# Value-score products in 128x32 tiles for four of six chunks, a second load of the values, and a new order of steps

## The chip, the cores and the metric

The kernel runs on one core of one Trainium2 chip. The metric is device time in microseconds (us), the median of the runs shown. A profile is one execution, taken by the hardware profiler. Engines: PE is TensorE (PEld are its weight loads), DVE is VectorE, ACT is ScalarE, POOL is GpSimd, SP is SyncE, which here only issues transfers.

## The reference

A gated recurrence over time feeds a bilinear feed-forward layer:

```python
# q, k, v, alpha: (B, H, S, D) = (4, 8, 768, 48)
for t in range(S):
    state = alpha[:, :, t, :, None] * state + np.einsum('bhd,bhe->bhde', k[:, :, t], v[:, :, t])
    y[:, :, t] = np.einsum('bhd,bhde->bhe', q[:, :, t], state)
x = y.transpose(0, 2, 1, 3).reshape(3072, 384)
out = ((x @ w_a) * (x @ w_b)) @ w_out          # w_a, w_b: (384, 1536), w_out: (1536, 384)
```

Everything comes in and goes out in float32; the large products use bf16.

## The kernel before

The work is cut into six chunks. Chunk `c` holds two of the four batches (`u` is 0 or 1 for them) and 256 time steps, as 128 pairs of neighbouring tokens, one pair per partition. A token's place in its pair is its rank (`rk` 0 or 1). Each 256 steps are again two halves `g` of 64 partitions, with a state passed from half to half.

For a chunk the steps are, by the names of the program:

- `ld a/k/q/v`: loads. `ln` (`logs`, L556) takes the logarithm of alpha, `l2` adds the two of a pair, `R`, `H` and `L` split it for exact sums, `B`, `A2` or `AQ` build running sums on PE, `E` (`expo`, L667) makes exponentials of them (`E u i` the inverse), `ra` (L645) another exponential, `lv` (`level`, L652) multiplies the first token of each pair, `mk`/`mq` (L678) scale keys and queries into `QKp`.
- `C` turns `QKp` on PE with `Ce` as its copy out (L742 on ACT, L744 on DVE); later chunks turn by a DMA transpose, `T` (tile `kqT`). `dk`/`de` (L721) or `dr`/`dl` make the decays.
- `v` (`vcast`, L785 on ACT, L787 on DVE) copies the loaded values into the padded tile `vx`; `K`, `K2` (L799, L812) are the state products and `k` the state update.
- `D` (L841) makes the scores. `M` masks them on DVE while copying out of PSUM; `Mc` copies on ACT (L850) and `Mm` masks in place later (L854).
- `SB` and `SA` (`carried`) add the states' part of the output, `Y` (`inner`) the products of values with masked scores; both issue at L865 in 64x64 tiles. The result lies in two PSUM banks, one per half `g`. `X` (`evac`, L900 on ACT, L902 on DVE) copies it as `xT`.
- The feed-forward layer: `a f w bank` and `b f w bank` (`ff`, L919) are three matmuls each into the bank that is named, for slice `f` of 12, over one `u` (256 columns) or both (`*`, 512 columns). `as` (L925) copies an `a` result out on ACT, which frees its bank; `pr` (L933) multiplies it with the `b` result on DVE, which frees that bank. `o m half bank` (L941) is six matmuls of 384 columns with `w_out`; `ot` copies out, `st` stores.

A `Y` of one `u` is 48 matmuls: 12 pieces (a head's 48 outputs cut at multiples of 64) times two ranks times two halves. Each contracts 64 partitions and gives 64 output rows for 128 columns; four tiles of 64x64 are used in turn.

No scheduler orders the work. `PROGRAM` is a written list of all steps, chunk number first, and each engine executes its instructions in the order of that list; steps of chunk `c+1` and `c+2` stand between the feed-forward steps of chunk `c`. PE, ACT, DVE, POOL and SP each have such a queue, and a waiting instruction holds up all behind it on its engine. All PSUM banks are named by hand, so a matmul into a bank waits for the copy of what the bank held.

The step `c1a` (`const_table`, L468) loads ACT's function table `natural_log_exp_and_others`, which holds logarithm, exponential and copy. It is the first thing that ACT does.

Of the kernel before, what the change touches and what calls it, by code (L numbers as in the profile page):

```python
# [17 lines left out]
0: cm 0; c1; cz 0 b P; ci; ld a 0b Y; c1a; ld a 0a Y; ln 0b; cu; cz 1 b P; fill 7 2; cu2 V; cz 0 q V; cus; ld k 0b Y; ld k 0a Y; B 0b 5; ld q 0b Y; ld v 0 P  # L18
0: ln 0a; ld q 0a Y; E 0b b; E 0b i; mq 0b V; B 0a 0; E 0a i; dk 0 2; E 0a b; ld a 1 P; mk 0b V; C 0 1 5; cs 0 m P; ld k 1 P; ld q 1 P; v 0 S; mk 0a V; cm 1
0: de 0; fill 2 1; mq 0a V; C 0 0 3; Ce 0 1 V; W b 0 256; cz 0 v P; Ce 0 0 V; D 0 1 4; ln 1; ld v 1 P; W a 256 768; K 0 0 6; k 0 0 V; M 0 1; D 0 0 0; SB 0 6  # L20
0: cz 1 q P; B 1a 2; M 0 0; W a 0 256; E 1a i; E 1a b; W b 256 768; mq 1a V; mk 1a V; B 1b 4; dk 1 3; E 1b i; E 1b b; de 1; v 1 S; mq 1b V; mk 1b V; C 1 0 0
0: Y 0; SA 0; Ce 1 0 V; cs 1 m P
1: ld a 0 P; ld a 1 P
0: W a 768 1536; C 1 1 1; X 0 S; c2 P; D 1 0 3; W b 768 1536
1: ld q 0 P
0: Ce 1 1 V; K 1 0 5; k 1 0 V; a 4 0 0
1: ld k 0 P
0: D 1 1 6; SB 1 1
1: ld v 0 P; ld q 1 P
0: Mc 1 0; a 3 0 5; Wo 0 6; a 0 0 3; Mm 1 0 V; Mc 1 1; as 0 0; b 0 0 4  # L30
1: ld k 1 P
0: pr 0 0; b 1 0 6; a 2 0 3; a 1 0 7; a 5 0 4; as 2 0; b 2 0 3; Mm 1 1 V; as 1 0; b 4 0 7; as 5 0; b 5 0 4; pr 2 0; pr 1 0
1: ln 0
0: SA 1; Y 1; Wo 6 12; K 1 1 6; as 3 0; as 4 0; X 1 S
1: ra 0
0: K 0 1 3
1: l2 0 V
0: b 3 0 0; pr 5 0; pr 4 0
1: H 0 V; L 0 V
0: a 2 1 1; a 5 1 2; as 5 1; pr 3 0; a 1 1 7; b 4 1 5; b 5 1 4; as 2 1; k 0 1 V; pr 5 1; a 4 1 2; as 1 1  # L40
1: ln 1
0: b 2 1 0; pr 2 1; a 6 * 3; as 4 1; b 1 1 2
1: l2 1 V
0: pr 4 1; as 6 *
1: H 1 V
0: pr 1 1
1: A2 0 7
0: a 11 * 0; a 7 * 5; a 0 1 4
1: L 1 V
0: k 1 1 V  # L50
1: ra 1
0: as 11 *
1: lv 0 q V; E 0 i
0: as 0 1; b 6 * 0; b 11 * 3; a 8 * 4; pr 6 *; pr 11 *
2: ld a * P
0: b 0 1 1; as 8 *; a 3 1 6
1: E 0 b; lv 0 k V
0: a 10 * 2; pr 0 1
1: mq 0 V; ld v 1 P
0: b 8 * 4  # L60
1: A2 1 7
0: as 10 *; b 10 * 2; pr 8 *
1: E 1 b
0: as 3 1; as 7 *; b 9 * 3; b 3 1 0; b 7 * 1; a 9 * 6
2: ld q * P
1: v 0 S; lv 1 q V; mk 0 V
0: pr 10 *
1: mq 1 V; C 0 1 4
0: as 9 *
1: C 0 0 2  # L70
0: o 0 0 5; pr 7 *
1: dk * 6
2: ld k * P
3: ld v * P
0: cz 1 v P; pr 9 *
1: Ce 0 0 S; E 1 i; de *; lv 1 k P; Ce 0 1 V; D 0 1 1; D 0 0 3
0: pr 3 1
1: Mc 0 0; K2 0 0 7 0
0: o 1 0 6
1: mk 1 V; M 0 1  # L80
0: o 3 0 4; o 1 1 -; ot 1 S; c3 P
3: ld a * P
0: cs 1 0 P; o 3 1 -
1: k 0 0 V; k 0 1 V; Mm 0 0 V; SB 0 1; C 1 0 3; C 1 1 7
0: ot 3 S; o 0 1 -
1: Ce 1 0 V
2: ln *
1: v 1 V; D 1 0 3; Ce 1 1 S; K2 1 1 6 0; Y 0; SA 0
0: ot 0 V
1: k 1 0 V; D 1 1 6  # L90
0: o 2 0 5
1: M 1 0
2: l2 0 V
1: X 0 S; a 3 0 1; Mc 1 1
2: l2s 0 P; l2s 1 P
1: a 2 0 3; a 4 0 4
2: R 0
1: k 1 1 V; as 4 0
2: ra 1
1: as 3 0; b 4 0 7  # L100
0: o 2 1 -
1: as 2 0
0: ot 2 S
1: pr 4 0
2: R 1; lv 1 q P
1: b 3 0 6; b 2 0 7; a 5 0 2; pr 3 0; b 5 0 3; as 5 0; b 1 0 5; a 1 0 1; pr 5 0; pr 2 0; a 7 0 2; as 1 0; pr 1 0
2: AQ 3
1: SB 1 6
2: lv 0 k P
1: a 10 0 5  # L110
2: lv 1 k V; ra 0; ld v * P
1: Mm 1 1 V
2: E 1 b
1: as 10 0; b 10 0 0; pr 10 0
2: mq 1 V; E 1 i
1: as 7 0; b 7 0 1
2: E 0 b; E 0 i
1: a 0 0 5
0: st 3 Y
2: dr  # L120
1: SA 1; Y 1
2: mk 1 V
1: pr 7 0; a 11 0 0; a 6 0 3; b 6 0 2; X 1 S; b 11 0 4; a 2 1 6; as 6 0; a 3 1 7; as 11 0; b 2 1 1; pr 6 0
2: lv 0 q V
1: b 4 1 0; as 2 1
2: T 1
1: pr 11 0
2: dl
0: st 0 Y
1: a 0 1 2; pr 2 1  # L130
2: mq 0 V
1: b 3 1 3; b 0 0 6; as 3 1; as 0 0; b 0 1 7; pr 3 1; a 8 0 1; a 9 0 5
0: st 1 Y
1: b 8 0 3; b 9 0 4; pr 0 0; as 0 1
2: mk 0 V
1: a 4 1 2
3: ln *
1: a 9 1 6; pr 0 1; as 8 0; b 9 1 1
3: ra 1
1: b 10 1 7; pr 8 0; a 10 1 3; as 4 1; as 9 0; as 9 1; a 6 1 6; b 6 1 2; b 11 1 5; pr 4 1; as 10 1; pr 9 0; a 11 1 4; pr 10 1; pr 9 1; as 6 1  # L140
2: v 1 S
1: a 8 1 3; b 8 1 1; a 7 1 6; pr 6 1
3: l2 0 V
1: as 11 1
2: T 0
1: as 8 1; a 5 1 4
3: ra 0
1: as 5 1; a 1 1 2
2: v 0 V
4: ld a * Y  # L150
1: pr 11 1; as 7 1; pr 8 1
2: K2 * * 0 7; D 1 1 3; D 1 0 5
1: as 1 1; b 5 1 2; o 2 0 1
2: k * 0 V
1: pr 5 1
3: v 0 S; v 1 S
1: b 1 1 2
2: Mc 1 0; M 1 1
3: l2s 0 P; l2s 1 P
1: b 7 1 0; o 2 1 -; pr 1 1; o 3 0 4  # L160
2: SB 0 5
1: pr 7 1
3: R 0
2: D 0 0 2
1: ot 2 V
2: Mm 1 0 V
1: o 3 1 -
2: Mc 0 0; SB 1 0; D 0 1 2
3: R 1
1: ot 3 S  # L170
2: SA 0
1: o 0 0 4
0: cs 0 0 P
2: Mc 0 1
4: ln *
3: ld q * Y; ld k * Y
2: k * 1 V
3: AQ 2
2: Y 1; SA 1; Mm 0 1 V; Mm 0 0 V; Y 0; X 0 S
3: E 0 b  # L180
4: l2 0 V
2: X 1 V
1: o 0 1 -
2: b 1 * 6; a 1 * 5
3: E 1 b
4: ld k * Y
3: E 1 i
1: ot 0 S
3: E 0 i
4: l2s 0 P  # L190
2: a 0 * 0; b 0 * 1; as 0 *; as 1 *
3: lv 0 k P; lv 0 q P
2: a 5 * 7
1: st 3 Y
2: a 7 * 4
4: l2s 1 P
2: a 2 * 5
3: lv 1 q V; mq 1 V; lv 1 k V
2: pr 1 *
3: dr  # L200
2: pr 0 *
3: mk 0 V
4: ld q * Y
0: st 2 Y
2: as 5 *; a 6 * 6; b 6 * 2; as 7 *
3: mq 0 V
2: b 9 * 4; b 7 * 0
1: st 2 Y
3: dl
4: R 0  # L210
2: b 5 * 7
1: o 1 0 3
2: a 9 * 1; pr 7 *; as 6 *
3: T 0
2: pr 6 *
4: ra 0
2: pr 5 *; a 11 * 6
3: mk 1 V
2: as 9 *; a 3 * 0
4: lv 0 k V; lv 0 q V; R 1  # L220
2: as 2 *
1: o 1 1 -
2: as 11 *; a 8 * 5; b 11 * 2; a 4 * 7; b 2 * 1
3: T 1
1: ot 1 V
2: pr 9 *; as 8 *; pr 11 *; pr 2 *; b 8 * 3; b 4 * 5; as 4 *
5: ld a * Y
3: K2 * * 4 6
2: pr 8 *; as 3 *; pr 4 *
3: k * 0 V; D 0 0 2; Mc 0 0  # L230
2: b 3 * 1
4: ra 1
2: pr 3 *; b 10 * 5; a 10 * 0
3: D 1 0 1; D 1 1 3
2: as 10 *
3: k * 1 V; Mc 1 1
2: o 0 0 7; o 2 0 0
3: M 1 0
5: ln *
2: pr 10 *  # L240
4: lv 1 q P
3: SB 1 3; D 0 1 1; Mc 0 1
4: lv 1 k P
5: ld q * Y
1: st 0 Y
3: SB 0 5
2: o 2 1 -
3: Mm 1 1 V; Mm 0 0 V; Mm 0 1 V
4: ld v * P
2: ot 2 S; o 0 1 -  # L250
4: AQ 0; E 0 b; E 0 i
3: SA 0; Y 0; SA 1
4: E 1 b
3: Y 1
5: l2s 1 V
4: mq 0 V; mk 0 V
3: X 0 S; X 1 S
2: o 3 0 2; o 3 1 -
4: T 0
3: a 5 * 3  # L260
4: E 1 i; v 0 S
3: a 9 * 0
2: ot 3 S
3: b 5 * 6; a 6 * 5; as 5 *
2: st 2 Y
3: as 9 *
5: ld k * P; l2s 0 P
3: as 6 *
5: ra 1
4: mq 1 V  # L270
2: ot 0 S
3: a 0 * 1
4: mk 1 V
3: a 1 * 2
4: D 0 0 3
5: l2 0 V
1: st 1 Y
4: dr
5: R 0
3: pr 5 *  # L280
4: v 1 S; M 0 0
3: b 1 * 7; as 1 *; a 3 * 5; b 9 * 6; pr 9 *; b 6 * 4; a 2 * 0; pr 6 *
4: T 1
5: lv 0 k P
3: b 0 * 6; as 0 *; as 2 *
4: dl
3: a 8 * 1
5: lv 1 q P
3: b 4 * 0; a 4 * 4; b 2 * 3; pr 1 *; pr 0 *; as 8 *; pr 2 *; as 4 *; pr 4 *; b 3 * 6; b 8 * 2
5: ld v * P; lv 1 k P  # L290
3: a 11 * 1
5: ra 0
3: as 3 *; pr 8 *; as 11 *; a 7 * 0
4: D 1 0 3; K * 0 5
5: lv 0 q P
3: pr 3 *; as 7 *
5: v 1 V
4: k * 0 V
5: R 1
4: D 1 1 6; D 0 1 1; Mc 1 0; Mc 1 1; M 0 1  # L300
2: o 1 0 0; o 1 1 -
3: a 10 * 7; b 11 * 3
4: SB 1 4
2: ot 1 S
3: as 10 *
4: Mm 1 0 V
3: pr 11 *
4: SB 0 1
5: AQ 6; E 0 i; E 0 b; mk 0 V
3: b 10 * 0; b 7 * 3  # L310
4: Mm 1 1 V
5: mq 0 V
3: o 2 0 6; pr 7 *
4: Y 0; SA 0
3: pr 10 *
5: E 1 b
4: X 0 V; Y 1; SA 1
2: st 1 Y
3: o 1 0 3
4: X 1 S  # L320
3: o 2 1 -
5: E 1 i
4: a 7 * 2
5: mq 1 V
4: b 7 * 7; a 6 * 1; as 7 *; as 6 *
3: o 1 1 -
4: b 1 * 5; a 0 * 1; a 1 * 4
5: dr; T 0
2: st 3 Y
4: b 6 * 2  # L330
3: ot 2 V
4: pr 7 *; a 5 * 6
5: mk 1 V
3: ot 1 V
4: pr 6 *
5: v 0 S
4: as 0 *; as 1 *; pr 1 *
2: st 0 Y
5: T 1
4: b 0 * 7; as 5 *; pr 0 *; a 4 * 1; a 3 * 0  # L340
5: K * 0 2; dl
# [757 lines left out]
```

## Time and profile before

| | |
|---|---|
| runs | 194.41 us median of 3 (193.69 to 194.47) |
| span of the profiled execution | 192.0 us (first to last instruction; the page gives no other time of it) |
| PE busy | 186.8 us, 97% |
| DVE / ACT / POOL busy | 133.1 / 106.5 / 56.9 us |
| granted PE clock | 1.000 |
| DMA | 62618 packets, 29.40 MB |
| last matmul group | starts at 187.17 us |

Busy times of one engine's instructions may overlap: a matmul's mean of 217 ns is its time from entering to leaving, while the next ones follow some 14 ns apart. What a stage costs is therefore read from starts: from the first instruction of a group to the first of the next.

### The profile page before, as it was taken

The numbers are of one execution on the slowest core, as the hardware profiler recorded it, in microseconds if no ns is written. First come the engines' busy times: TensorE is split into PE (matmuls) and PEld (weight loads), VectorE is DVE, ScalarE is ACT, GpSimd is POOL, SyncE is SP. The second block draws the span as 40 slices with busy tenths as digits, with TensorE's granted clock in tenths as the row PEclk, the third lists the DMA queues.
The fourth block names the chain that finished last, engine by engine and source line by source line (L and its number), as shares of the span: only waits on it lengthen the run. The fifth ranks groups of instructions, "written<-read, shape, count | busy, mean of one in ns | idle before, by whom it ended". The sixth has DMA issues, their size and how long they took to land.

```text
span 192.0 us, 6086 instructions
## 1 busy us (share of the span) xinstructions
PE 186.8 (97%) x2613; PEld 116.9 (61%) x2613; DVE 133.1 (69%) x223; ACT 106.5 (55%) x194; POOL 56.9 (30%) x75
## 2 busy tenths in 40 slices
PE   7999999999999999999999999999999999999992
PEld 3888875677778876645557444656465644545562
DVE  2387698994989888899897956887567446252510
ACT  4448885656779867753487756743572435314211
POOL 8999626752450500640074262000000000000000
PEclk9999999999999999999999999999999999999999
DMA  5999999999969999999999989017641200000422
GB/s 132 274 219 218 251 253 235 244 269 264 251 107 166 165 216 265 248 254 149 233 213 181 156 174 129 3 42 140 146 66 44 85 0 0 0 0 3 164 82 82
DMA packets 62618, 29.40 MB, mean 153 GB/s; under 512 B 53712, under 2 KB 60768, under 8 KB 62592
## 3 DMA queue, kind: packets, MB, share of 16 engines
q0 software_dynamic: 18432, 13.37, 39.6%
q1 hardware_dynamic: 44016, 15.55, 38.1%
q8 instruction: 20, 0.33, 0.7%
q10 hardware_dynamic: 144, 0.10, 0.2%
q14 instruction: 6, 0.05, 0.1%
HBM read 25.98 MB, written 4.74 MB: 160 GB/s over the span
## 4 chain that ended last, share of the span: by engine, by line
PE 91%; DMA 5%; SPq 1%; DVE 1%; issue 1%; ACT 0%; DVEq 0%
PE psum L919 47%; PE psum L941 24%; PE psum L865 7%; PE psum L841 3%; DMA kqT<-QKp 3%; DMA q_t<-in_q_dram 3%; PE psum L736 2%; PE psum L633 1%; PE psum L952 1%; SPq L549 1%; PE psum L799 1%; PE psum L812 1%; PE psum L700 1%; PE psum L591 1%; PE psum L592 1%
## 5 line engine op out<-in xcount | busy, mean ns | idle before, releaser
L919 PE MATMUL psum<-xT,wb_t 128*128 128x512 bf16 (+1 forms) x270 | 56.0, 337 | 0.0
L919 PE MATMUL psum<-xT,wa_t 128*128 128x512 bf16 (+1 forms) x270 | 56.0, 337 | 0.0
L941 PE MATMUL psum<-wo_t,prod 128*128 128x384 bf16 x276 | 49.4, 326 | 0.0
L919 PEld LDWEIGHTS <-wb_t 128*128 128x128 bf16 x270 | 25.9, 98 | 19.9 <-issue 0.5
L919 PEld LDWEIGHTS <-wa_t 128*128 128x128 bf16 x270 | 25.9, 98 | 19.7 <-issue 0.3
L941 PEld LDWEIGHTS <-prod 128*128 128x128 bf16 x276 | 25.9, 98 | 17.6
L956 ACT ACTIVATE ot<-psum 128x384 f32<-128x384 f32 (+1 forms) x16 | 7.7, 482 | 22.7 <-PE psum L941 21.6
L850 ACT ACTIVATE m<-psum 128x1024 bf16<-128x1024 f32 x14 | 14.1, 1023 | 4.6 <-PE psum L841 4.3
L613 POOL TENSOR_TENSOR l<-la 64x384 f32<-64x384 f32 x7 | 7.8, 1108 | 26.6 <-ACT la L556 19.0
L846 DVE TENSOR_TENSOR m<-psum,mask 128x1024 bf16<-128x1024 f32 x10 | 12.1, 1220 | 3.1 <-PE psum L841 3.1
L652 POOL TENSOR_TENSOR q_t<-q_t,ra 128x384 f32<-128x384 f32 x5 | 6.1, 1215 | 22.5 <-ACT ra L645 19.7
L556 ACT ACTIVATE la<-a_t 128x1536 f32<-128x1536 f32 (+2 forms) x9 | 9.5, 1055 | 2.3 <-DMA a_t<-in_alpha_dram 2.2
L678 DVE TENSOR_TENSOR QKp<-q_t,beta 128x768 bf16<-128x768 f32 x10 | 10.0, 995 | 1.0 <-ACT beta L667 1.0
L865 PE MATMUL psum<-m,vx 64*64 64x128 bf16 x576 | 10.5, 217 | 0.0
L900 ACT ACTIVATE xT<-psum 128x768 bf16<-128x768 f32 x9 | 7.2, 816 | 5.7 <-PE psum L865 5.5
L678 DVE TENSOR_TENSOR QKp<-k_t,invb 128x768 bf16<-128x768 f32 x10 | 9.7, 972 | 0.8 <-ACT invb L667 0.8
L854 DVE TENSOR_TENSOR m<-m,mask 128x1024 bf16<-128x1024 bf16 x14 | 9.3, 684 | 1.2 <-ACT m L850 1.2
L958 DVE COPY ot<-psum 128x384 f32<-128x384 f32 (+1 forms) x9 | 4.8, 532 | 7.6 <-PE psum L941 4.7
L865 PEld LDWEIGHTS <-vx 64*64 64x64 bf16 x576 | 9.0, 107 | 0.5 <-issue 0.3
L841 PE MATMUL psum<-kqT 64*64 64x128 bf16 x384 | 9.0, 219 | 0.4 <-DMA kqT<-QKp 0.3
L652 POOL TENSOR_TENSOR k_t<-k_t,a_t 128x384 f32<-128x384 f32 x6 | 7.4, 1228 | 6.1 <-issue 3.3
L549 POOL DMA_DIRECT2D v_t<-in_v_dram x8 | 8.5, 1058 | 0.1
(271 smaller groups left out, 287.9 us busy)
## 6 DMA issues: line engine op xcount, KB each, us to landing
out_dram<-ot SPq DMA_DIRECT2D x23, 192.0 KB, 3.8
q_t<-in_q_dram SPq DMA_DIRECT2D x3, 768.0 KB, 6.5
a_t<-in_alpha_dram POOLq DMA_DIRECT2D x2, 768.0 KB, 15.2
k_t<-in_k_dram POOLq DMA_DIRECT2D x2, 768.0 KB, 12.1
v_t<-in_v_dram POOLq DMA_DIRECT2D x4, 384.0 KB, 7.0
a_t<-in_alpha_dram SPq DMA_DIRECT2D x2, 768.0 KB
k_t<-in_k_dram SPq DMA_DIRECT2D x2, 768.0 KB
a_t<-in_alpha_dram POOLq DMA_DIRECT2D x3, 384.0 KB, 8.5
```

Source lines behind the costliest of these rows:

```text
L549: eng.dma_start(out=t[:, us, hs].rearrange("p b h r d -> p (b h) (r d)"), in_=src[ch.b0 + us.start:ch.b0 + us.stop, hs, ch.s * 2 * C:(ch.s ...
L556: nc.scalar.activation(out=ch.la[:, us, hs].rearrange("p b h r d -> p (b h r d)"), in_=ch.a[:, us, hs].rearrange("p b h r d -> p (b h r d) ...
L613: eng.tensor_add(ch.l2[(1 - g) * HC:(2 - g) * HC, 1], x[:, :, 0, :], x[:, :, 1, :])
L652: eng.tensor_mul(x, x, by)
L678: eng.tensor_mul(QKp[ch.c % 2][:, u, j, :, hs, :D], src[:, u, hs].rearrange("p h r d -> p r h d"), f)
L841: nc.tensor.matmul(s2[g * HC:(g + 1) * HC, r, p, rk, :], lhsT=turned_part(ch, u, 1, rk, 2 * h + p, g, rs), rhs=queriesT(ch, u, 2 * h + p, ...
L846: nc.vector.tensor_mul(m.rearrange("p r a k s -> p (r a) (k s)"), ch.s2[u, h].rearrange("p r a k s -> p (r a) (k s)"), maskn(4))
L850: nc.scalar.activation(out=m.rearrange("p r a k s -> p (r a) (k s)"), in_=ch.s2[u, h].rearrange("p r a k s -> p (r a) (k s)"), func=AF.Copy)
L854: eng.tensor_mul(x, x, maskn(4))
L865: nc.tensor.matmul(y[c * DP:(c + 1) * DP, g, j // 2 * C:(j // 2 + 1) * C], lhsT=lhsT, rhs=rhs, start=(g, c) not in begun, stop=False, skip ...
L919: nc.tensor.matmul(p, lhsT=(wa_t, wb_t)[w][:, kk, f * 128:(f + 1) * 128], rhs=ch.xT[:, kk, us, :], start=(kk == 0), stop=(kk == KT - 1))
L941: nc.tensor.matmul(op, lhsT=ch.prod[:, f, at:at + C], rhs=wo_t[:, f, :], start=(f == 0), stop=(f == NFF - 1))
```

## The change

For chunks 2 to 5 (`NR = 2`), `Y` contracts over both ranks at once: 64 pairs times two ranks are 128 partitions, and an output piece is 32 rows, so the tiles are 128x32, four of them side by side. A `Y` of one `u` is then 16 slices times two halves, 32 matmuls, still of 128 columns. In all 256 matmuls stand where 384 were; chunks 0 and 1 keep theirs (192).

- The scores `D` of these chunks write their halves and ranks in the other arrangement (as many matmuls), with the mask `mask2`, built once from `mask` (`cm2`).
- `lw` (`load_rows`) loads the values a second time in that layout, into a reshaped view of `vx`: four loads per chunk on POOL's queue, 16 in all, each of 64 x 16 pieces of 48 elements. `cz 0 w` and `cz 1 w` zero the padding. `ld v` stays, for the state products, which now read it directly; `vcast` is gone for these chunks (nine on ACT and three on DVE become three and one).
- `evac` copies one half `g` at a time (24 copies of 128x384 in place of 12 of 128x768; ACT 13, DVE 11) and puts the tokens in their own order, so that `ff_prod` reads and writes without a permutation.
- `PROGRAM` is new throughout. Among much else, six `l2` additions move from DVE to POOL, three more of the `lv k` multiplications too, two more `Ce` copies go to ACT, and `Y` and `SA`/`SB` are grouped: over the whole program PE changes its tile size 58 times where it did 55 times.
- `c1a` now stands late in chunk 1's steps. The built program has 11 table loads on ACT where it had one: besides `c1a` itself, one ahead of `ln` in five places, and one ahead of `E` or `ra` in five places, in each case directly before that instruction in ACT's order.

The core of the diff, with the lines of the new list that matter here:

```diff
-0: cm 0; c1; cz 0 b P; ci; ld a 0b Y; c1a; ld a 0a Y; ln 0b; cu; cz 1 b P; fill 7 2; ...
+0: c1; cm 0; cz 0 b P; ci; cu; cu2 V; cus; ld a 0b Y; fill 7 0; ln 0b; B 0b 2; cz 1 b P; ...
+0: ... v 0 S; cs 0 m P; Ce 0 1 V
+0: C 0 0 1; Ce 0 0 V; cz 1 v P; ld k 1 P; K 0 0 2; de 0; ... SB 0 2; ln 1; W b 0 256; B 1a 6; E 1a i
...
+0: K 1 1 2; D 1 1 6; Mc 1 1; k 1 1 V; SB 1 0; a 0 0 3; as 0 0
+1: ld a 1 P
+0: b 0 0 4; a 3 0 5; b 1 0 2; a 1 0 6; as 1 0; a 4 0 3; as 4 0; Mm 1 0 V; Mm 1 1 V; Y 1; SA 1; W a 768 1536; X 1 1 S; X 1 0 V; pr 0 0; b 4 0 3; b 5 0 6; a 2 0 7
+0: b 1 1 0
+1: ln 0
+0: a 0 1 1; c2 P; W b 768 1536; as 0 1; pr 1 0; a 1 1 2; as 1 1; pr 4 0
+1: ld q 0 P
+0: a 5 0 4; as 5 0; b 0 1 1; pr 0 1; b 3 0 2; b 5 1 3
...
+0: o 3 1 -
+1: Mc 0 0
+2: ln *; l2s 1 P
...
+2: R 0; ra 1
+1: v 1 S; K2 1 1 6 7; k 1 0 V
+2: R 1
+1: Ce 1 0 S
...
+0: o 1 0 1
...
+1: b 5 0 3; b 10 0 4; a 11 0 5; pr 0 0; pr 10 0
+2: lw 0 0 P
+1: as 5 0; pr 5 0
+3: ln *
+1: X 1 0 V; b 9 0 2; b 3 0 1; as 9 0; a 2 0 6; as 2 0; a 4 0 4
...
+1: b 0 1 0; pr 9 0; a 2 1 7
...
+3: ra 1
...
+1: b 11 0 2; as 4 0; pr 4 0
+3: lw 0 0 P
+1: a 0 1 3; a 4 1 4; as 4 1; ...
...
+0: c1a; cz 0 w P
...
+    VP = D + DP // 2
+    NR = 2
...
+    vps = [t.rearrange("p b r h e -> p (b r h e)")[:, :4 * H * VP].rearrange("p (g b h e) -> p g b h e", g=2, b=2, h=H) for t in vxs]
...
+    def load_rows(ch, g, rk, eng):
+        at = ch.s * 2 * C + g * C
+        eng.dma_start(out=vps[ch.c % 2][rk * HC:(rk + 1) * HC, g, :, :, :D].rearrange("p b h d -> p (b h) d"),
+                      in_=v[ch.b0:ch.b0 + 2, :, at:at + C, :].rearrange("b h (s r) d -> r s (b h) d", r=2)[rk])
...
+    def values(ch, gs, u, rk, hd):
+        return ch.v[gs, u, hd, rk, :] if ch.c >= NR else vxs[ch.c % 2][gs, u, rk, hd, :D]
...
+    SLICES = [(h, 3 * (h // 2) + j) for h in range(H) for j in ((0, 1) if h % 2 == 0 else (1, 2))]
+    RANKS = [[x for x in SLICES if x[1] % 4 == c] for c in range(4)]
+
+    def inner_rows(ch, u):
+        y, begun = ch.y[u]
+        vp = vps[ch.c % 2].rearrange("p g b h e -> p g b (h e)")
+        W32 = DP // 2
+        for n in reversed(range(len(SLICES) // 4)):
+            for g in range(2):
+                for c in range(4):
+                    h, j = RANKS[c][n]
+                    at = h * VP + W32 * j - D * h
+                    nc.tensor.matmul(y[c * W32:(c + 1) * W32, g, j // 4 * C:(j // 4 + 1) * C], lhsT=vp[:, g, u, at:at + W32],
+                                     rhs=ch.m[u, h // 4][:, h % 2, h // 2 % 2, g, :], start=False, stop=False, skip_group_check=True)
+
     def inner(ch, u):
+        if ch.c >= NR:
+            return inner_rows(ch, u)
...
-    def evac(ch, u, eng):
+    def evac(ch, u, g, eng):
...
-        o_ = ch.xT[:, :, 2 * u:2 * u + 2, :].rearrange("p a g s -> p g a s")
-        i_ = ch.y[u][0][:, :, :KT * C].rearrange("p g (a s) -> p g a s", a=KT)
...
+        evict(ch.xT[:, :, 2 * u + g, :].rearrange("p a (s r) -> p a r s", r=2),
+              ch.y[u][0][:, g, :KT * C].rearrange("p (a r s) -> p a r s", a=KT, r=2), eng)
...
-        o_, a_, b_ = tokens(ch.prod[:, f, :], us), columns(a[:, :n], n), columns(b, n)
-        nc.vector.tensor_mul(o_, a_, b_)
+        nc.vector.tensor_mul(ch.prod[:, f, us.start * C:us.stop * C], a[:, :n], b)
```

## The prediction

> **What bounds the kernel now.** First the page: busy times, the slices, the chain.
>
> ```profile
> PE 186.8 (97%) x2613; PEld 116.9 (61%) x2613; DVE 133.1 (69%) x223; ACT 106.5 (55%) x194; POOL 56.9 (30%) x75
> ...
> PE   7999999999999999999999999999999999999992
> ...
> DMA  5999999999969999999999989017641200000422
> ...
> PE 91%; DMA 5%; SPq 1%; DVE 1%; issue 1%; ACT 0%; DVEq 0%
> ```
>
> PE carries the chain and has work in every slice after the first. What PE waited for, from the waits of PE alone, is almost nothing:
>
> ```profile
> PE psum L574 <- DVE og L472: 1.2, 1, 1.2
> PE psum L841 <- DMA kqT<-QKp: 0.3, 1, 0.3
> ```
>
> So a matmul less is time gained, and any new wait of PE is time lost, one for one: nothing gives it back. Prices are steps between starts. From the chain in order of time (start, length, what):
>
> ```profile
> 49.72 1.31 PE psum L919 x12
> ...
> 86.91 0.98 PE psum L941 x6
> ```
>
> 1.31/12 = 0.109 us per matmul of 256 columns, so 0.33 us for an `a` or `b` of one `u`; 0.98/6 = 0.163 us for 384 columns. From PE's timeline:
>
> ```profile
> 127.94 1.14 PE L941 MATMUL psum<-wo_t,prod 128*128 128x384 bf16 x6
> 129.01 0.87 PE L865 MATMUL psum<-m,vx 64*64 64x128 bf16 x48
> ...
> 129.87 0.84 PE L865 MATMUL psum<-m,vx 64*64 64x128 bf16 x48
> 130.54 0.22 PE L865 MATMUL psum<-kqT,S 64*64 64x128 bf16 x1
> ```
>
> The second `Y` takes 130.54 - 129.87 = 0.67 us: 14 ns per 64x64 matmul, 56 ns per four. A change of tile size costs 129.01 - 127.94 - 6 x 0.163 = 0.09 us. Last ACT, at the start and by groups:
>
> ```profile
> 0.73 1.28 ACT L468 ACT_TABLE_LOAD   x1 [0.73 <-PEq L1083]
> 3.62 1.14 ACT L556 ACTIVATE la<-a_t 128x384 f32<-128x384 f32 x2 [1.61 <-DMA a_t<-in_alpha_dram]
> 6.68 0.87 ACT L667 ACTIVATE prod<-psum 128x384 f32<-128x384 f32 x2 [1.92 <-PE psum L592]
> ...
> 10.80 0.84 ACT L556 ACTIVATE la<-a_t 128x768 f32<-128x768 f32 x1 [0.43 <-DMA a_t<-in_alpha_dram]
> ```
>
> ```profile
> L556 ACT ACTIVATE la<-a_t 128x1536 f32<-128x1536 f32 x4 | 5.9, 1476 | 0.0
> ...
> L700 PE MATMUL psum<-og,la 128*48 128x2 f32 x64 | 1.8, 186 | 0.0
> ```
>
> A table load is 1.28 us of ACT, and today's single one lies under the wait for alpha.
>
> **The products.** 384 matmuls become 256, each still of 128 columns. If four 128x32 tiles run side by side as four 64x64 tiles do, the step stays 14 ns: 128 x 14 ns = -1.8 us. No row has a 128x32 tile. The lower end is this price. For the upper end, L700 is the only row with full-height, column-cut tiles: 32 of them step at 26 ns (14.83 to 15.67 us), by which 256 cost 6.7 us against 5.4: +1.3. I take 14 ns: L700's weights are float32, and its streams are two columns.
>
> A rule that speaks against the edit: L941's weight loads take 98 ns each, all on the same 128 rows, and still its matmuls follow each other at 163 ns for 384 columns, so these loads hide. The Trainium skill (TensorE: Matmul & The Clock Gate, Part 3, The mechanism) says that a weight load overlaps running matmuls only where the row group differs, though it names the background buffer as a second way; 128-row tiles share all row groups. What exposed loads would cost stands below as a rival.
>
> Tile sizes change 58 times for 55: 3 x 0.09 = +0.3.
>
> **The table loads** are the largest term. With `c1a` late, ten more are put ahead of `ln`, `E` and `ra`, directly in ACT's queue, and behind each wait the `as` that free PE's banks. At each I ask which PE step needs the next ACT step. `as` is 0.38 us (128x256), `la` 0.84 or 1.48, `ra` and `E` 0.5.
> - Loads 1, 2 and 4, chunk 0: 1 replaces today's; 2 ends at 4.76 + 1.28 = 6.0, before PE delivers at 6.68; 4 lies under the wait for `B 1a`. Nothing.
> - Load 3 (`ln 1`, chunk 0) starts when `de 0` ends, 10.38, and ends at 11.66, so `la` starts there and not at 10.80. All up to the first feed-forward matmul hangs on it: +0.9.
> - Load 5 (`ln 0`, chunk 1). From the end of `SA 1`, ACT does `X` 0.5 and 0.2 of lag, the load 1.28, `la` 0.84, `as 0 1` 0.38: 3.2. `b 0 1 1` goes into the bank that `as 0 1` empties, and PE has seven `a`/`b` before it, 2.3: +0.9. Without the load ACT needs 1.9, no wait.
> - Load 6 (`E 0 i`, chunk 1): `as 10` and `pr 10` come 0.25 late for `a 2 1 1`: +0.25.
> - Loads 7, 8 (`ln *`, `ra 1` of chunk 2). Counted from the end of the scores `D 0 1`, ACT has `Mc` 1.0, load, 1.5, load, 0.5, `v 1` 0.85: done at 6.4, and `K2 1 1`, which reads it, is due at 5.85: +0.6. `Ce 1 0` takes another 1.0, and `o 1 0 1` goes into its bank: +0.6 more.
> - Loads 9, 10 (`ln *`, `ra 1` of chunk 3). Counted from the end of `SA 1` of chunk 1, ACT ends `as 5 0` at 0.3, the load 1.6, `la` 3.1, `as 9 0` 3.4; `a 2 1 7` needs that bank at 2.9: +0.5. Then `as 2 0`, the load, `ra`, `as 11 0`, `as 4 0` end at 6.3; `a 4 1 4` is the fourteenth and due at 13 x 0.33 + 0.5 = 4.8: +1.5.
> - `c1a` itself: `as 10 1` 0.1 late for `b 10 1`: +0.1.
>
> Sum +5.4. Below: 0, if PE has reserves here that I don't see. Above: eight of these loads in full, 8 x 1.28 = 10.3.
>
> **What lies beside.**
> - `lw`: 16 issues at POOL's 1.06 us (L549) are 17 us on an engine 30% busy, but `l2` and `lv k`, now also there, queue behind them, and chunk 1's `l2 0` holds the loads behind it on POOL until `la` is there. Transfers: 16384 packets, at 22 to 36 ns (the trace's 384-byte and v packets) over 16 engines 23 to 37 us more on queues that have 149 us now and are busy to 115 us. Rows bound it: a turning transfer takes 5.0 us after issue, and `lw` is issued some 15 us ahead of its `Y`. I take 0; above, +2 if `T` or chunk 2's alpha comes late.
> - `X` in halves: 24 of about 0.5 us (as `ot`) on two engines at once where 12 of 0.82 to 0.95 stood; `vcast` gives ACT 6 x 0.85 = 5.1 back; `pr` without a permutation, `l2` off DVE: all on engines that PE doesn't wait for. 0, with -0.5 as lower end for the shorter `X`.
>
> **Sum.** Span 192.0 - 1.8 + 0.3 + 5.4 = 195.9. The median of the runs, 194.4, is 2.4 above the profile's span; I keep that: 198.3 us. What can be told from no change here is 0.5%, 1.0 us.
>
> **Rivals.**
> - *The gain stays.* PE's banks and ACT's spare 45% swallow the loads; then -1.8 + 0.3, and up to -0.5 for the shorter `X`: 192.4 to 192.9. It decides where all loads together cost PE under 0.5 us (1.5 is the break-even). For it: ACT is the engine with most idle time after POOL. Against: ACT's idle time is not where the loads are; from 60 to 70 us ACT is busy 9.08 of 10 us, the stage of loads 9 and 10.
> - *Half of it.* The waits are half as long since steps behind a stalled PE catch up: 2.7 - 1.5 = +1.2, near the line; 193.5 to 195.4.
> - *A table load costs more than its row.* After today's load ACT idles 1.61 us, put down to DMA; anything hidden in it would now show. Eight exposed loads x 1.61 = +12.9 at most: up to 211, and 203 at a third of it. The Trainium skill (ScalarE: Activation LUTs, What ACT_TABLE_LOAD costs) gives 1283 ns, as our row, and a further drain of about 1380 ns for each switch. By that figure the sum would be near 209, an estimate. No row here shows the drain.
> - *Column tiles take turns.* Weight loads or streams in the same rows don't overlap: each product then takes the 56 ns that four take now, 256 x 56 = 14.3 for 5.4, +9: 207. Against it: the L941 steps above, and L700 at 26 ns.
>
> **How the numbers follow.** Forecast 0.60 (196 to 202); gain stays 0.16; half of it 0.12; dearer loads 0.07; turns 0.05. Slower by over 0.5%: 0.60 + 0.07 + 0.05 = 0.72. Same: 0.12. Faster: 0.16. The range leaves out about one in ten at each end: 193.0 takes in part of the first rival, 203 the forecast with its transfers late and a third of the drain. Without the other sign the forecast's own range is 196 to 202.
>
> **What would show it.** Right: 11 table loads of 1.28 us; PE waits of 0.5 us or more at the `a`/`b` named, put down to ACT's `as`, mostly within 20 to 80 us, summing to 3 to 7 us; PE back to back after that; a `Y` pair of chunks 2 to 5 of 64 matmuls in 0.9 us. Wrong: PE's slices without waits and a span near 190.5 (loads hidden); a `Y` pair of over 1.6 us (tiles don't overlap); `la` starting over 1 us after its load without a transfer to wait for (drain); PE waiting for `vx` or `kqT` by DMA (the new loads).

## The result, and the profile after

The changed kernel takes 212.13 us in the median (210.99 to 216.15, four runs) against 194.19 us for the kernel before (193.69 to 194.47): a ratio of 1.091, 95% interval 1.086 to 1.096. It is slower, as forecast, but by 18 us and not by 4; 212.1 lies outside the range of 193 to 203. Ratios and intervals, here and below, leave out runs in the slower state that this chip sometimes shows (a lower granted clock, like the 0.958 of the run of 216.15 us); the medians are of all runs. The profiled execution has a span of 209.2 us against 192.0.

The page of the changed kernel, the lines that answer to those shown of before: busy time, PE's and DMA's slices, the chain.

```profile
PE 188.9 (90%) x2469; PEld 116.6 (56%) x2485; DVE 134.6 (64%) x218; ACT 115.7 (55%) x204; POOL 82.1 (39%) x104
...
PE   7997899998968999996877799689999999999993
...
DMA  6999999999999999997999858997570300000224
...
PE 56%; DMA 18%; POOL 7%; DVE 6%; issue 6%; ACT 5%; SPq 1%; POOLq 0%; DVEq 0%; ACTq 0%
```

PE has holes in a dozen slices, and the chain is no longer PE's own: 18% of it are transfers. What PE waited for (total, times, longest):

```profile
PE psum L828 <- DMA kqT<-QKp: 4.7, 2, 2.5
PE psum L916 <- DVE prod L929: 2.9, 3, 1.9
PE psum L916 <- DVE xT L954: 1.4, 2, 0.9
...
PE psum L885 <- issue: 1.1, 1, 1.1
PE psum L718 <- DVE QKp L660: 0.9, 1, 0.9
PE psum L797 <- ACT vx L767: 0.7, 1, 0.7
PE psum L916 <- ACT as__1294 L922: 0.6, 1, 0.6
```

Where the prediction looked for ACT's `as`, the two first rows are the turning transfers and DVE's `prod`; all waits for ACT, two of five rows shown, are 2.4 us together, and `as` has 0.6 of it. Of the 17.2 us by which the span grew, 15.1 are time in which PE is idle, and 2.1 are busy time, though the program has 128 matmuls fewer; a part of that is a stretch at half clock, of which more at the end. The new product itself does what was forecast, from PE's timeline, the pair of `Y` of chunk 2 and the first carried product behind it:

```profile
83.36 1.08 PE L885 MATMUL psum<-m,vx 128*32 128x128 bf16 x64
84.37 0.24 PE L854 MATMUL psum<-kqT,S 64*64 64x128 bf16 x1
```

84.37 - 83.36 = 1.01 us for 64 matmuls, which follow each other at 13.6 ns, and the changes of tile size around them; two 64x64 `Y` took 2 x 0.67. And the table loads, from ACT's timeline:

```profile
10.36 1.28 ACT L538 ACT_TABLE_LOAD   x1
11.65 0.84 ACT L538 ACTIVATE la<-a_t 128x768 f32<-128x768 f32 x1
```

The load takes 1.28 us, as its row of before, and `la` starts 0.01 us after its end; the activation ahead of the load ended at 10.34 us, 0.02 us before it.

### The profile page after: what moved, and what is told of

Read it like the earlier page. It is cut to its first block, busy times and chain, and to the rows that moved or that the text cites. A ratio compares the mean times of both kernels' runs of the same rounds, so it can differ in the third digit from the quotient of the medians.

```text
span 209.2 us, 5843 instructions
## 1 busy us (share of the span) xinstructions
PE 188.9 (90%) x2469; PEld 116.6 (56%) x2485; DVE 134.6 (64%) x218; ACT 115.7 (55%) x204; POOL 82.1 (39%) x104
## 4 chain that ended last, share of the span: by engine, by line
PE 56%; DMA 18%; POOL 7%; DVE 6%; issue 6%; ACT 5%; SPq 1%; POOLq 0%; DVEq 0%; ACTq 0%
PE psum L916 31%; PE psum L937 17%; DMA kqT<-QKp 6%; DMA a_t<-in_alpha_dram 5%; DMA bl<-row 4%; DMA v_t<-in_v_dram 3%; DVE QKp L660 3%; PE psum L854 2%; PE psum L885 2%; DVE prod L929 2%; PE psum L828 2%; PE psum L615 1%; ACT la L538 1%; PE psum L948 1%; POOL q_t L526 1%
## 5 line engine op out<-in xcount | busy, mean ns | idle before, releaser
L839 ACT ACTIVATE m<-psum 128x1024 bf16<-128x1024 f32 x14 | 14.2, 1025 | 13.3 <-PE psum L828 13.3
L634 POOL TENSOR_TENSOR k_t<-k_t,a_t 128x384 f32<-128x384 f32 x9 | 11.5, 1276 | 10.2 <-issue 5.8
L952 ACT ACTIVATE ot<-psum 128x384 f32<-128x384 f32 (+1 forms) x15 | 6.9, 469 | 14.2 <-PE psum L937 13.0
L531 POOL DMA_DIRECT2D vx<-in_v_dram x16 | 13.3, 841 | 0.0
L660 DVE TENSOR_TENSOR QKp<-k_t,invb 128x768 bf16<-128x768 f32 x10 | 11.9, 1190 | 1.7 <-ACT invb L649 1.3
L660 DVE TENSOR_TENSOR QKp<-q_t,beta 128x768 bf16<-128x768 f32 x10 | 10.9, 1085 | 1.9 <-ACT beta L649 1.9
L952 ACT ACTIVATE xT<-psum 128x384 bf16<-128x384 f32 x13 | 7.3, 601 | 7.3 <-PE psum L854 4.8
L828 PEld LDWEIGHTS <-kqT 64*64 64x64 bf16 x384 | 6.8, 111 | 7.7 <-DMA kqT<-QKp 5.2
L843 DVE TENSOR_TENSOR m<-m,mask 128x1024 bf16<-128x1024 bf16 x14 | 10.1, 742 | 0.2
L546 POOL TENSOR_TENSOR l<-la 128x384 f32<-128x384 f32 x6 | 6.2, 1036 | 7.1 <-ACT la L538 6.9
L954 DVE CAST xT<-psum 128x384 bf16<-128x384 f32 x11 | 6.0, 580 | 4.3 <-PE psum L854 4.3
## 6 DMA issues: line engine op xcount, KB each, us to landing
out_dram<-ot SPq DMA_DIRECT2D x23, 192.0 KB, 2.1
```

The lines of the kernel that those rows point to most:

```text
L531: eng.dma_start(out=vps[ch.c % 2][rk * HC:(rk + 1) * HC, g, :, :, :D].rearrange("p b h d -> p (b h) d"), in_=v[ch.b0:ch.b0 + 2, :, at:at + ...
L634: eng.tensor_mul(x, x, by)
L660: eng.tensor_mul(QKp[ch.c % 2][:, u, j, :, hs, :D], src[:, u, hs].rearrange("p h r d -> p r h d"), f)
L828: nc.tensor.matmul(s2[half * HC:(half + 1) * HC, r, p, part_, :], lhsT=turned_part(ch, u, 1, rk, 2 * h + p, g, rs), rhs=queriesT(ch, u, 2 ...
L839: nc.scalar.activation(out=m.rearrange("p r a k s -> p (r a) (k s)"), in_=ch.s2[u, h].rearrange("p r a k s -> p (r a) (k s)"), func=AF.Copy)
L843: eng.tensor_mul(x, x, maskn(ch, 4))
```

## The experiments

Theory T is the prediction's: the table loads cost. Rival R: the second loads of the values do. Rival O: the new order of the steps does, whichever product runs in it. Each kernel was timed beside the kernel before on the same chip; that one stayed between 193.9 and 194.2 us in every comparison.

### Tables, second loads, products

*table_first*: the table is loaded once, in the first step.

```diff
-0: c1; cm 0; cz 0 b P; ...
+0: c1; c1a; cm 0; cz 0 b P; ...
-0: c1a; cz 0 w P
+0: cz 0 w P
```

> The changed kernel with one step moved: c1a (the table that holds logarithm and exponential) is loaded as ACT's first act, so the ten other table loads fall away (12.8 us of ACT). Theory tables: PE's new waits between 20 and 70 us come from ACT held up by loads, some 5 to 6 us of the 17 lost, and the waits after 90 us stay: about 207 us. Rival order: the waits come from how the steps are placed, and the loads only lie beside them: 211 us or more. Rival cascade: the late waits, too, follow from the early ones: under 200 us.

Measured: 211.51 us, ratio 1.090 (1.087 to 1.092). One table load in the trace instead of eleven, and the time is that of the changed kernel within the intervals: as the cause of the lost 18 us, T falls. The loads did hold PE up, though, about as the working had it. Without them PE stands 2.0 us earlier behind the turn `C` of chunk 0 (17.43 us for 19.41), and 2.9 us earlier at 55 us (55.04 us for 57.94); the waits at 51 us (0.9 and 0.36) are gone. By 64.5 us this lead is lost (64.50 for 64.52). A stall inside chunk 0's `Y 1` that the changed kernel has as well, with 0.44 us,

```profile
23.98 0.86 PE L854 MATMUL psum<-m,vx 64*64 64x128 bf16 x47 [0.44 <-issue]
```

grew to 1.67 us. At 57 to 61 us PE waits 3.0 us for DVE's `xT`, where the changed kernel waits 3.05 in four pieces up to 67 us (from start to start; by the profile's idle times 2.7 and 2.4). And from 61.0 to 64.4 us the clock was granted at 0.51. So the time of the loads was covered and not free.

*no_reload*: the changed kernel without its sixteen `lw` (chunks 2 to 5 multiply stale values). *table_first_no_reload*: both edits.

> The changed kernel without the 16 second loads of the values (chunks 2 to 5 then multiply what lies in the tile). Theory reload: the waits after 90 us (turning transfers late by 2.6 and 2.3 us, DVE slow beside POOL 2.9, a throttled stretch 1.1) come from the 16384 extra packets and from POOL: 8 to 10 us less, about 203 us. Rival order: the packets find room, and the waits stay: 210 to 212 us.

> Both edits at once. If tables and reload are two separate causes, the gains add up: 212 - 5 - 9 = about 198 us, and what is left over 192.7 (before less 1.5) is the new order's own. Rival order: over 206 us.

Measured: 208.03 us, ratio 1.070 (1.066 to 1.073), and 206.94 us, 1.065 (1.062 to 1.068). By the ratios, R holds for 4 to 5 of the 18 us: the wait for `kqT` at 108 us (2.6) is gone without the loads. The second one, behind 130 us, is still there in no_reload (2.4), and so is the larger part of the time.

*products_only*: the order of before, with the 128x32 products, the scores' new arrangement and `mask2`; no second loads, so chunks 2 to 5 multiply stale values.

```diff
+    NR = 2
...
+        if ch.c >= NR:
+            return inner_rows(ch, u)
...
-0: cs 1 0 P; o 3 1 -
+0: cm2 P; cs 1 0 P; o 3 1 -
```

> The kernel before, its order and its table load kept, with the products of chunks 2 to 5 in 128x32 tiles, the scores in the other arrangement and the second mask; the values are not loaded a second time (the products read what lies in the tile), and vcast stays. Theory side by side: 128 matmuls less at 14 ns, -1.8 us, and up to 0.9 back for more changes of tile size: 192.6 to 193.5 us. Rival turns: tiles in the same rows don't overlap, +9 us, 203 us.

Measured: 193.71 us, ratio 0.998 (0.996 to 0.999). The products follow each other at 13.3 ns, so 128 fewer are 1.7 us; but in the old order each `Y` stands beside a 64x64 `SA`, and PE changes its tile size 67 times instead of 55: 12 x 0.09 = 1.1 us given back, an estimate. The products in this form can't be where 18 us come from.

*order_only*: the reverse, the new order with 64x64 products, no second loads, table first (the casts of chunks 2 to 5 left out, and `Y 0` ahead of `Y 1` in chunk 5).

```diff
-    NR = 2
+    NR = 6
-5: Y 1; Y 0; SA 0; SA 1; X 1 0 V; ...
+5: Y 0; Y 1; SA 0; SA 1; X 1 0 V; ...
```

> The changed order of steps alone: values of all chunks multiplied as before in 64x64 tiles, no second loads, the table loaded once at the start; two products of chunk 5 swapped (Y 0 before Y 1). The casts of the values of chunks 2 to 5 are left out, so those chunks multiply the values of chunks 0 and 1. Theory 'the order costs': 207 to 209, that is the 206.9 of table_first_no_reload plus the 1.5 that the products bring. Rival 'the new products cost, though only in the new order': under 200.

Measured: 208.03 us, ratio 1.067 (1.060 to 1.074). O holds: 13 to 14 of the 18 us come with the order, where neither the new products nor the second loads are left. The copies `X` in halves and the missing casts are still in this kernel; no run took them out alone.

### What in the order costs

In the slices around 95 us PE waits for `prod`. DVE's timeline of the changed kernel there, then POOL's, then PE's:

```profile
92.35 1.73 DVE L660 TENSOR_TENSOR QKp<-k_t,invb 128x768 bf16<-128x768 f32 x1
94.00 1.75 DVE L660 TENSOR_TENSOR QKp<-q_t,beta 128x768 bf16<-128x768 f32 x1
95.67 1.75 DVE L660 TENSOR_TENSOR QKp<-k_t,invb 128x768 bf16<-128x768 f32 x1
97.35 0.68 DVE L929 TENSOR_TENSOR prod<-as__1848,psum 128x512 bf16<-128x512 bf16 x1
```

```profile
92.25 1.01 POOL L546 TENSOR_TENSOR l<-la 128x384 f32<-128x384 f32 x1
93.21 1.73 POOL L634 TENSOR_TENSOR k_t<-k_t,a_t 128x384 f32<-128x384 f32 x1
```

```profile
95.39 0.81 PE L916 MATMUL psum<-xT,wb_t 128*128 128x512 bf16 x3
98.07 2.10 PE L916 MATMUL psum<-xT,wb_t 128*128 128x512 bf16 x8 [1.88 <-DVE prod L929]
```

Three `QKp` in a row take 1.73 to 1.75 us. Beside the first, and the first half of the second, POOL runs `l2` and `lv k`, steps that DVE had before; beside the third POOL does not run a tensor step but issues loads (95.35 to 98.19 us), and what slowed that one is not shown. The same operation takes 0.95 us in the rows of before at 84.6 and 88.2 us, where POOL is busy 0.86 of 10 us. The `prod` that frees PE's bank stands behind them.

*pool_back*: table_first with every `l2`, `l2s` and `lv` on its engine of before. *pool_back_no_reload*: the same without the second loads.

```diff
-1: l2 0 P; H 0 V
+1: l2 0 V; H 0 V
...
-4: l2 0 P; lv 0 k P; R 0
+4: l2 0 V; lv 0 k V; R 0
```

> table_first with every l2, l2s and lv on the engine that it had before (eleven steps go back from POOL to DVE, four the other way). Theory 'POOL's tensor work slows DVE and delays the operands of the turning transfers': QKp on DVE goes back from 1.75 to 0.95 us, the PE waits at 95 us (prod, 2 us) and for kqT (2.5 and 2.7 us) go, 204 to 208. Rival 'it is where the steps stand, whoever does them': 210 to 213, or more, since DVE has 10 us more to do.

> pool_back without the sixteen second loads (chunks 2 to 5 multiply stale values). Theory 'POOL is the common cause': what the second loads cost (4 us) and what the tensor work costs are the same queue, and both gone gives 198 to 203. Rival 'where the steps stand': 206 to 208, as table_first_no_reload.

Measured: pool_back 208.95 us (205.1 to 209.8), too scattered for a verdict. pool_back_no_reload 202.56 us, ratio 1.044 (1.040 to 1.049), against 1.065 for table_first_no_reload: -4.0 us. The three `QKp` are back at 0.95 us and no wait for a turned `kqT` by DMA is left. But the wait for `prod` at 96 us is still there, 2.6 us: the moved steps now stand on DVE in a row between two `prod`s, and one step of that row, `lh`, takes 1.75 us beside a load's issue and then a tensor step on POOL. So it is shown that these steps on POOL cost 4 us and that the `QKp` are slow with them; that the 4 us come through the speed of DVE is in part argued. The stall at 96 us has a second cause, the row of DVE steps, and the granted clock differs too (0.982 to 0.983 in the three runs behind the one ratio, 0.989 to 0.999 in the four behind the other).

*x_behind*: pool_back_no_reload with the copies `X` of chunks 0 and 1 written behind the next three feed-forward products. PE's timeline of pool_back_no_reload, behind chunk 1's `Y 1` and `SA 1`:

```profile
58.21 0.28 PE L905 MATMUL psum<-xT,wb_t 128*128 128x256 bf16 x1
59.53 0.71 PE L905 MATMUL psum<-xT,wb_t 128*128 128x256 bf16 x5 [1.04 <-DVE xT L943]
```

`b 5 0` reads the rows of `u` 0, long there, and yet from its second matmul on it waits for `X 1 1`, which writes those of `u` 1: the order in which the steps are written makes it wait, not what it reads.

```diff
-1: Y 1; SA 1; X 1 1 V
-2: dl; ra 0; lv 0 q V
-1: b 5 0 3; b 10 0 4; a 11 0 5; pr 0 0; pr 10 0
+1: Y 1; SA 1; b 5 0 3; b 10 0 4; a 11 0 5; X 1 1 V; X 1 0 S
+2: dl; ra 0; lv 0 q V
+1: pr 0 0; pr 10 0
```

> pool_back_no_reload (202.6) with the X steps of the second unit of chunks 0 and 1 written behind the next three feed-forward products instead of ahead of them, both X of chunk 1 side by side. In the trace those products start one matmul and then wait for X, although they read the other unit's rows. Theory 'a product written behind X waits for all of X': the waits at 23.6, 58.2 and 60.4 us (0.65, 1.2 and 1.1) shrink to under 0.4 each, 199.5 to 201. Rival 'DVE and ACT are late there, whatever the order on PE': 202 to 203.

Measured: 201.80 us, ratio 1.042 (1.037 to 1.047), not told apart from pool_back_no_reload's 1.044. The wait for `X` did go:

```profile
58.57 0.83 PE L905 MATMUL psum<-xT,wb_t 128*128 128x256 bf16 x6
59.24 0.49 PE L905 MATMUL psum<-xT,wa_t 128*128 128x256 bf16 x3
61.05 0.81 PE L905 MATMUL psum<-xT,wb_t 128*128 128x256 bf16 x6 [1.32 <-ACT as__1246 L911]
```

Nine matmuls run at once, and then PE waits 1.3 us for ACT's `as`, which the added `X` on ACT holds up. The mechanism was right, the gain was not: ACT and DVE are both late there.

*x_behind_spread*: x_behind, with five DVE steps of chunks 3 and 4 spread over the next `prod`s.

```diff
-4: l2 0 V; lv 0 k V; R 0
 2: b 2 * 0; b 7 * 4
-4: lv 0 q V
 2: pr 2 *
+4: l2 0 V
...
+4: lv 0 k V; R 0
...
+4: lv 0 q V
```

> x_behind, and the DVE steps l2, lv k, R and lv q of chunk 4, and mk 1 of chunk 3, which stand in a row between two prods of chunk 2, are spread over the next five prods. Theory 'DVE's steps in a bunch hold up prod and by it PE': the wait of 2.7 us for prod at 96 us goes, 2 to 3 us less than x_behind. Rival 'DVE is short over the whole stage': the same time as x_behind, the wait moves to the next prods.

Measured: 200.68 us, ratio 1.036 (1.033 to 1.038): 1.1 us, not 2 to 3. The wait of 2.6 us for `prod` at 96 us is gone (0.5 left), so the row of steps did hold up PE; but a wait of 1.7 us for `kqT` stands at 102.6 us: PE comes to this product 5 us earlier than in x_behind, where it started at 107.82 us, and its turning transfer is issued only 1.3 us earlier (93.81 us for 95.14). Of PE's waits that before did not have, the largest six rows there have 0.7 to 1.7 us each (`kqT` by DMA 1.7, `as` 1.3, `prod` 1.1, `xT` 0.7, issue 1.2 and 0.8), in sum 6.8, about the 7.0 by which its span, 198.9, is above that of products_only, 191.9. This rest was not taken apart further.

### Waits without a cause in the profile

In table_first, as in the changed kernel, PE stops twice inside a `Y` for "issue", that is for nothing that the profile shows: in chunk 0's `Y 1`, and in the `Y` pair of chunk 3.

```profile
21.29 0.24 PE L854 MATMUL psum<-m,vx 64*64 64x128 bf16 x1
23.20 0.86 PE L854 MATMUL psum<-m,vx 64*64 64x128 bf16 x47 [1.67 <-issue]
...
115.87 0.63 PE L885 MATMUL psum<-m,vx 128*32 128x128 bf16 x31
117.78 0.68 PE L885 MATMUL psum<-m,vx 128*32 128x128 bf16 x33 [1.29 <-issue]
```

The first comes after 350 matmuls of PE's program, the second 1278 later. The instruction queue moves packets of 16 KB; between the two stalls lie ten of them, and 2485 matmuls share 19, 131 each (the expectation below reckons with 128). Both stalls end 2.7 to 2.9 us after the start of such a packet (20.53 and 114.92 us). So do those of the changed kernel, 2.7 and 2.6 us after packets at 21.25 and 115.68 us: there PE reaches the first place 2.0 us later, and the stall is shorter for it.

*shifted*: table_first, with 21 more matmuls at PE's start.

```diff
-fill 7 0; ln 0b; B 0b 2
+fill 4 0; warm 24 0; ln 0b; B 0b 2
```

> table_first with 21 more matmuls on PE before the first real one (three of the seven 512-column fills at the start, 0.43 us each, become 24 of 128 columns), so that every later matmul stands 21 places further in PE's program and starts at the same time. It is for the two waits of PE inside a product that the profile puts down to 'issue': 1.85 us before the second matmul of chunk 0's Y 1, 1.45 us in the middle of chunk 3's Y pair, 1278 matmuls later, ten 16 KB packets of the instruction queue apart (10 x 128 = 1280). Theory 'PE waits for its instructions where such a packet begins': the first wait moves 21 matmuls forward, out of Y 1 into the feed-forward products before it, and shrinks to under 0.6 us, since these take 0.1 us each and cover the fetch; the second moves from after 31 to after about 10 matmuls of its Y pair. Rival 'something that these two Y wait for': both stay in their places.

Measured: 217.93 us of two runs, and 213.8 us in the profile, where the clock was granted at 0.959 against table_first's 0.984; the time says nothing here, the place does:

```profile
18.94 0.30 PE L854 MATMUL psum<-kqT,Sm 64*64 64x128 bf16 x4
21.56 0.24 PE L854 MATMUL psum<-kqT,Sm 64*64 64x128 bf16 x2 [2.32 <-issue]
```

The stall is at the same place in PE's program, after 349 matmuls in a trace that lacks the record of one before it, now in the middle of a carried product that waits for nothing, and it ends 2.4 us after a packet's start (19.17); the `Y 1` behind it runs through. That it would shrink was wrong: 21 places ahead of `Y 1` lies not yet a feed-forward product but the end of `SB 1`, as dense as `Y`. The second stall is gone instead of moved; its packet starts at 117.58 us, under an `o`, 2.6 us ahead of the pair. So the first stall belongs to a place in PE's program and not to what its product waits for. That PE waits there for its instructions fits all these numbers; no run took the fetch itself away, so it is argued and not shown. Before shows no such stall; its packet at 130.67 us, for one, starts as an `o` of 2 us begins.

### The change in the order of before

*old_order_grouped*: products_only, with the second loads in place of the casts, four in a row, and `SA 0; SA 1` side by side ahead of both `Y`.

```diff
+0: cz 0 w P
+2: lw 0 0 P; lw 0 1 P; lw 1 0 P; lw 1 1 P
...
-4: l2s 1 P
+4: l2s 1 P; lw 0 0 P; lw 0 1 P; lw 1 0 P; lw 1 1 P
...
-3: SA 0; Y 0; SA 1
+3: SA 0; SA 1; Y 0
```

> The change without its order: the order of before, products of chunks 2 to 5 in 128x32 tiles, the values of these chunks loaded a second time in place of the cast, four loads in a row on the POOL queue some 15 to 30 us ahead of the products; both carried products of a chunk stand side by side ahead of both 128x32 products, which takes away some of the tile-size changes. Theory 'the order costs': 192.5 to 194.5, a little under before at best, since the loads have POOL's idle stretches to themselves. Rival 'the second loads cost wherever they stand': 196 to 199, the 4 us that leaving them out gave in the new order, and PE waits for vx or kqT by DMA.

Measured: 199.41 us, ratio 1.026 (1.022 to 1.030): the rival's number. PE's largest wait is 2.1 us for an `xT` whose copy stands on DVE behind chunk 4's `l2`, and this behind an alpha load that SyncE issues at 68.47 us, in products_only at 66.32. SyncE's queue shows why PE waits for `kqT` as well, 2.1 us: the pair of turning transfers of chunk 3, first in products_only, then here, where the loads of chunk 4 go out at 87 us:

```profile
85.66 6.15 SPq L785 DMA_TRANSPOSE kqT<-QKp  x2
```

```profile
89.17 10.85 SPq L781 DMA_TRANSPOSE kqT<-QKp  x2
```

*old_order_late_loads*: the loads of chunk 2 at 42 us, of chunk 3 behind the landing of its last turning transfer (a small POOL copy waits for it), of chunks 4 and 5 behind chunk 4's transfers; chunk 2's `SA` and `Y` as before. *old_order_gate0*: chunk 3's loads 4 us earlier (92.15 us for 96.10). *old_order_245*: chunk 3 as before, with casts and 64x64 products.

```diff
+2: lw 0 0 P; lw 0 1 P; lw 1 0 P; lw 1 1 P
...
-3: T 1
+3: T 1; gatet 1
+0: cz 1 w P
+3: lw 0 0 P; lw 0 1 P; lw 1 0 P; lw 1 1 P
...
 5: lv 0 q P
+4: lw 0 0 P; lw 0 1 P; lw 1 0 P; lw 1 1 P
+5: lw 0 0 P; lw 0 1 P; lw 1 0 P; lw 1 1 P
```

> The order of before with the 128x32 products and the second loads, as old_order_grouped (199.4), but no second load is on the queues together with a turning transfer: those of chunk 2 at 42 us, of chunk 3 behind the landing of chunk 3's last turning transfer, of chunks 4 and 5 behind chunk 4's; carried products side by side in chunks 3 to 5 only. Theory 'the second loads cost where they run beside turning transfers and delay them': a pair of turning transfers of chunk 3 takes 6 us again, not 10.9, PE doesn't wait for kqT, 193 to 195. Rival 'the second loads cost through the volume on the queues': 196 to 199.

> old_order_late_loads (194.46) with the second loads of chunk 3 behind the landing of the first of chunk 3's two turning transfers, not the second: some 3 us earlier. The theory 'beside turning transfers' gives: PE's wait for vx at 104 us (0.8) goes, POOL's steps for chunk 4 are not held up (the kqT wait at 112 us, 1.0, goes), against a second turning transfer up to 2 us longer, which PE doesn't need yet: 192.5 to 193.9. Rival 'volume': 194 to 196.

> old_order_late_loads (194.46) with chunk 3 as before: 64x64 products with cast values; 128x32 products and second loads in chunks 2, 4 and 5 alone, whose loads stand where PE did not wait for them. Theory 'the second loads cost where other transfers that are due share the queues', that is chunk 3's: PE's waits for vx (0.8) and kqT (1.0) at 104 to 113 us go and three quarters of the 1.8 us stay: 192.8 to 193.8, at or just under before. Rival 'they cost everywhere': 194.2 to 195.

Measured: 194.46 us, ratio 1.003 (1.001 to 1.006); 195.51 us, 1.008 (1.007 to 1.010); 193.32 us, 0.997 (0.996 to 0.999). With the loads away from the turning transfers the pair takes 5.87 us again, and by the ratios 4.4 us of old_order_grouped are gone (chunk 2's `SA` and `Y`, moved back too, have a share in that which was not told apart). Chunk 3's loads stay a problem: PE waits 0.8 us for `vx`, and 2.0 us where they go out 4 us earlier. There the last of the four lands at 105.96 us, 11.3 us after its issue, where it took 6.6 us to 105.13. So, against the expectation, the place beside a turning transfer is not all: an alpha and a q load that SyncE issues at 91.78 and 92.86 us share the queues with them, and the q load, too, lands later (105.27 us for 101.75). Without chunk 3's second loads PE is back at 97%; old_order_245, busy times and then all that PE waited for:

```profile
PE 184.3 (97%) x2502; PEld 114.7 (60%) x2517; DVE 132.2 (69%) x221; ACT 103.5 (54%) x190; POOL 67.4 (35%) x91
```

```profile
PE psum L591 <- DVE og L475: 1.2, 1, 1.2
PE psum L753 <- DVE QKp L695: 1.0, 1, 1.0
PE psum L961 <- issue: 0.2, 1, 0.2
```

The second wait ends at 8.85 us, where before starts the same product at 8.94, so it costs nothing. Of the kernels that leave nothing out it is the one that beats both, before by 0.3% with twelve runs; this is under the 0.5% that the prediction named as what can be told from no change.

## Why the prediction was wrong

- **The sign and its ground** held: PE had no reserve, new waits went into the time one for one.
- **The products** held as a price (13.3 to 13.6 ns, 1.01 us a pair). That they save 1.8 us less 0.3 in the new order, where the tile sizes are grouped, is not shown: order_only and table_first_no_reload, which differ in the products, have ratios of 1.067 and 1.065, 0.5 us apart and within their intervals. In the old order 1.1 of it goes into tile changes, an estimate; 0.2% was measured.
- **The table loads**, the largest term, failed as a term of the sum, and not as local prices. The working priced the waits of the step behind each load as if that load were the only late thing there, and added them up to 5.4. PE's waits at 51 us (0.9 and 0.36) matched loads 7 and 8 (1.2) and went with them; at 58 us PE stands 2.9 us later with the loads than without, where the sum has 3.25 for them. Those at 57 to 67 us (3.05) matched loads 9 and 10 (2.0), but without the loads DVE's `xT` kept PE for 3.0 there. And the time fell by no more than the interval (1.091 to 1.090), since a longer stall in `Y 1`, the wait for `xT` and a stretch at half clock took the lead back. A wait that a sum finds at the right place and size need not be the only thing that is late there.
- **What lies beside** is the step that made the number wrong: priced at 0 with an end of +2, it was some 17 us. The runs put 13 of them into the order with its moves between engines, and 4 to 5 into the second loads. Of the order, -4.0 went when `l2` and `lv` were back on DVE, -1.1 for a row of DVE steps, and 7 are many small waits whose causes stay open.
- "All on engines that PE doesn't wait for" was the false sentence: `l2` and `lv k` are ahead of `QKp`, and DVE's `QKp` are ahead of the `prod` that frees PE's bank. The estimate for `lw` (23 to 37 us more on the queues, a turning transfer 5.0 us after issue) had the numbers in it; what it lacked is that a pair of turning transfers takes 10.85 us instead of 6.15 where `lw` go out beside it, in old_order_grouped, and that `T` came late for its own reasons as well.
- **Small readings.** A run's time is 1.7 to 2.1 us above the span of that run, where the sum took 2.4; an issue of `lw` takes 0.84 us of POOL and not 1.06. Neither matters beside 17 us.
- **Rivals.** The drain behind a table load (the Trainium skill, ScalarE: Activation LUTs, What ACT_TABLE_LOAD costs) isn't seen: 0.01 us between load and `la`. The estimate of 209 from it came near the time by accident. Column tiles don't take turns. "Gain stays" and "half of it" fall. No rival named the order itself, and none had 212.
- **The signs.** "PE waiting for `vx` or `kqT` by DMA" was listed as what would show it wrong, with the new loads as the reason, and it is the largest row of the waits; of its two waits only one went when the new loads were left out.

## What to carry to other kernels

When an order of steps is replaced, the order is the change: price every step that moves between engines and every row of steps that comes to stand ahead of what frees the bottleneck's buffers, and give "beside" a real upper end. Take one suspected cost out before believing its place in a chain; where several engines are late at once, removing one wait only shows the next. New small-packet loads belong where no transfer that is due shares the queues; of the kernels here with such loads, the one that kept to this is the one that lost nothing.

## What the runs showed of the hardware

- DVE beside POOL: a 128x768 multiplication of two operands in SBUF took 0.95 us alone, and 1.73 and 1.75 us at 92.35 and 94.00 us, where POOL ran tensor steps; `prod`, with one operand in PSUM, took 0.68 us beside such steps at 91.08 us. The Trainium skill (SBUF — State Buffer, Who interferes with whom) says that a DVE instruction with two SBUF inputs and a GpSimd instruction that reads SBUF contend for ports that they share, and calls these an exclusive lock. These two agree, and so does POOL's `k_t` step at 93.21 us, 1.73 us where the same step on `q_t` had 1.00 at 91.30. Which of the two began first seems to decide: a multiplication at 119.49 us took 0.97 us, and POOL's step that began 0.23 us behind it took 1.60. The third multiplication of the row, 1.75 us beside POOL's issues of loads alone, is not explained by this.
- Instruction fetch, as the likely cause: stalls of 0.4 to 2.3 us in dense stretches of PE's program, the first at a fixed place, each ending 2.4 to 2.9 us after the start of a 16 KB packet of the instruction queue. The Trainium skill (Runtime: NRT & Kernel Launch, Instruction fetch mechanics) gives blocks of 16 KiB, 256 instructions, that is 128 matmuls with their weight loads, as the packets here, and calls the crossing mostly hidden; if these stalls are crossings, in a stretch of matmuls 14 ns apart it was not.
- The clock: after the wait for `kqT` that ended at 136.3 us in the changed kernel, three 512-column matmuls took 1.48 us from 137.77 us, steps of 0.43 us where 0.22 is usual; the granted clock from 136.9 to 140.3 us was 0.50. That is a loss of up to 1.7 us on top of the wait, half of 3.4, an estimate. Not every wait is followed by it: after the one of 2.5 us that ended at 111.28 us the clock stayed at 1.00. So a comparison of two kernels that differ in their waits can hold some of this as well.
